# Attention sums and values as 64x32 products, eight side by side, with x in even and odd features

## The chip, the cores and the metric

The kernel runs on one core of one Trainium2 chip. The time is the device time of one execution in microseconds (us). Engines are TensorE (PE; PEld is its weight load), VectorE (DVE), ScalarE (ACT), GpSimd (POOL) and SyncE (SP), which only issues transfers.

## The reference

Windowed attention over 8 batches of 8 heads (576 positions, 64 features), and then a GEGLU feed-forward block over the 8 x 576 = 4608 tokens.

```python
scores = scale * q @ k.transpose(0, 1, 3, 2)            # [8, 8, 576, 576]
mask_plain = (rel >= 0) & (rel < 32)                     # heads 0 to 3
mask_dil = (rel >= 0) & (rel < 128) & (rel % 4 == 0)     # heads 4 to 7
attn = exp(scores - max) / sum                           # under the mask
x = (attn @ v).transpose(0, 2, 1, 3).reshape(4608, 512)
out = (gelu(x @ w_gate) * (x @ w_val)) @ w_out           # d_ff 1536
```

## The kernel before

*Attention.* Two heads form a pair, which fills the 128 partitions; pair n belongs to batch n // 4, and n % 4 is 0 or 1 for plain heads, 2 or 3 for dilated ones. The dilated heads' positions are sorted by their remainder modulo 4, so each head is a narrow band of blocks, 64 keys by up to 96 queries. For a pair these are the steps, each a letter in the kernel's programs:

- **S**: scores, keys on partitions, products of 64x64 tiles (K = 64 features, 64 keys) into PSUM. **P**: exp on ScalarE, of 832 columns for a plain pair and 768 for a dilated one. **M**: times a mask of zeros and ones on VectorE.
- **D**: sums of P over the keys, as products with ones in 64x64 tiles, so that each sum stands in 64 partitions. **N**: values, products with v. Row halves and column halves of the array give four tiles; a word such as `N20@10+N21@40` sends the products of two pairs in turn, so that four tiles can work side by side.
- **l** and **r**: the reciprocal of the sums on ScalarE, as Ln and then Exp of the negative. **X**: values times the reciprocal, on VectorE, into `xT`, the transposed x (features on partitions, four tiles of 128 features, `kc`).

Batch 0 is computed at the start; its first two pairs use 128x128 products with a block-diagonal v (`vdiag`) and block-diagonal ones (`two_ones`), and VectorE turns and inverts their sums (**T**, **B**).

*Feed-forward.* Tokens go in nine chunks of 512. A chunk has a gate phase (`gate_words`) of 96 products of 128x512: 12 blocks of 128 hidden features, each with four gate and four val products over the four `kc`. Gelu (**g**) runs on ScalarE, its product with val (**u**) on VectorE, which in chunks 1 to 8 also forms sums of u blocks (**k**) for a seven-product scheme. The out phase (`out_words`) has 48 products of 128x512 in chunk 0 and 84 of 128x256 in the others, and then **q**, **e** and **w**, which combine and store results through two buffers, `snap`, that lie in `vdiag`. The out phase of chunk c also holds the attention of batch c + 1 for c up to 6; chunks 7 and 8 have none.

*Order.* A program is a string of words; a bare number sends that many feed-forward products to TensorE, any other word sends a step to its engine. Each engine runs its instructions in the order written, and semaphores make it wait. `orders` says in which order the first 16 gate products of a chunk go (three digits: which of the first two blocks, gate or val, kc), so that those which need late parts of x come last. The out phases of chunks 2 to 5 end with the scores of two pairs of the next chunk's batch, so that chunks 3 to 6 find these done; in the out phases of chunks 1 and 2 all scores of their batch are computed.

*Weights.* GpSimd issues the loads of w_gate and w_val (`load_w`, with conversion to 16 bit) in four parts of hidden features, 256, 256, 512 and 512 wide (`WC`). The second pair of heads of batch 0 and the weights come while the start computes.

Of the kernel before, what the change touches and what calls it, by code (L numbers as in the profile page):

```python
# [9 lines left out]
F16 = mybir.dt.float16  # L10
# [11 lines left out]
def kernel(  # L22
# [50 lines left out]
    two_ones = const.tile([P, P], F16, tag="two_ones")  # L73
# [3 lines left out]
    WC = [(0, 256), (256, 512), (512, 1024), (1024, 1536)]  # L77
# [6 lines left out]
    vdiag = const.tile([P, 2 * NB2 * P], F16, tag="vdiag")  # L84
# [9 lines left out]
    snap = [vdiag.bitcast(F32)[:, DM * i : DM * i + DM] for i in range(2)] + [turned[:, 0:DM]]  # L94
# [58 lines left out]
    def load_w(*parts):  # L153

        for i in parts:
            for t, w in ((wg_t, moe_w_gate), (wv_t, moe_w_val)):
                src = w[:, WC[i][0] : WC[i][1]].rearrange("(kc p) n -> p kc n", p=P)
                nc.gpsimd.dma_start(out=t[i], in_=src)
# [35 lines left out]

    diag = vdiag.rearrange("p (e c) -> p e c", c=P)

    def zero():

        for x in range(2):
            nc.vector.memset(at2(vdiag[64 * x : 64 * x + 64].bitcast(F32), 32 - 32 * x, [[64, 2 * NB2], [1, 32]]), 0.0)  # L200
# [32 lines left out]
    def load_v(b, i, plain):  # L233

        st = st_of(i)
        for g in range(2 * plain):
            for x in range(2):
                rows_ = v[b, 2 * g + x].rearrange("(j p) d -> p j d", p=64)
                dst = st[half_of(x, b and g), 576 * g : 576 * g + 576].rearrange("p (j d) -> p j d", j=NB2)
                gated(nc.sync.dma_start(out=dst, in_=rows_))  # L240
        for g in range(2 - 2 * plain):
            for x in range(2):
                half = st[half_of(x, g), 576 * g : 576 * g + 512]
                rows_ = v[b, HK + 2 * g + x, 0 : 4 * P].rearrange("(i p r) d -> p i (r d)", i=2, r=4)
                nc.sync.dma_start(out=half.rearrange("p (i c) -> p i c", i=2), in_=rows_)
        for x in range(2 - 2 * plain):
            dst = st[half_of(x), 512:1152].rearrange("p (g c) -> p g c", c=64)[:, 0:10:9]
            heads = slice(HK + 1, HK + 3) if x else slice(HK, HK + 4, 3)
# [6 lines left out]
    def cast_diag(g):  # L255

        st = st_of(0)[:, 0:1152].rearrange("p (e d) -> p e d", d=D)
        at = slice(NB2 * g, NB2 * g + NB2)
        for x in range(2):
            nc.gpsimd.tensor_copy(diag[half_of(x), at, half_of(x)], st[half_of(x), at])  # L260
# [4 lines left out]

    def odd(n):

        return n % 2 if n >= NHP else 0
# [32 lines left out]
    def cast_part(b, plain, behind=None):  # L301

        ins = cast_v(views(b)[5 - plain], 2 - plain)
        if behind is not None:
            tc.add_manual_dep(ins.ins, behind.ins.name, SYNC, reason="masks first")

    def v_cast(b, g, rest=False):

        dst = views(b)[5][:, NB2 * g : NB2 * g + NB2]
        for x in range(2):  # L310
            half = half_of(x, b and g)
            nc.gpsimd.dma_start(
                out=dst[half, 0:8].rearrange("p (i r) d -> p i (r d)", r=4),
                in_=v[b, HK + 2 * g + x, 0 : 4 * P].rearrange("(i p r) d -> p i (r d)", i=2, r=4),
            )
            if rest:
                heads = slice(HK + x, H, 2)
                if b:
                    heads = slice(HK + 1, HK + 3) if x else slice(HK, HK + 4, 3)
# [5 lines left out]
    def v_cast_plain(b):  # L325

        for g in range(2):
            dst = views(b)[4][:, NB2 * g : NB2 * g + NB2]
            for x in range(2):
                rows_ = v[b, 2 * g + x].rearrange("(j p) d -> p j d", p=64)  # L330
                nc.gpsimd.dma_start(out=dst[half_of(x, g)], in_=rows_)
# [15 lines left out]
    def pair(n):  # L347
        return (n + 2 * (n // NHP in (2, 3))) % NHP

    def is_plain(n):  # L350
        return pair(n) < NHP // 2
# [54 lines left out]
    def win(n, at):  # L406

        bank, kind = at // 10, at % 10
        return 512 * bank + ((0, 832, 960, 0) if is_plain(n) else (80, 880, 880, 64))[kind]

# [33 lines left out]
    def emit(mms):  # L444
        for o, lhs, rhs, st, end in mms:
            nc.tensor.matmul(o, lhs, rhs, start=st, stop=end, skip_group_check=True)  # L446

    def emit_tiles(*lists):

        queues, at = [list(mms) for mms, _ in lists], [0.0] * len(lists)  # L450
        while any(queues):
            i = min((i for i in range(len(lists)) if queues[i]), key=lambda i: at[i])
            o, lhs, rhs, st, end = queues[i].pop(0)
# [23 lines left out]
    def two_s(n, bank):  # L477
# [4 lines left out]
        emit_tiles((two_s_mms(n, bank, not biased), odd(n)))  # L482
# [110 lines left out]
    def two_a(n):  # L593
        two_l(n)
        two_r(n)
# [446 lines left out]
```

## Time and profile before

| | |
|---|---|
| median of 3 runs | 319.06 us (318.95 to 319.46) |
| the profiled execution, its own time | 318.66 us |
| its span, first to last instruction | 317.0 us |
| granted TensorE clock | 1.0 |
| TensorE products | 3489, busy 310.8 us |

The profile comes from one execution; its span leaves out 1.7 us of that execution's own time. "PE" rows count a product from its start to its modelled end, so neighbours overlap; distances are read from start to start. A row such as `PE L457 MATMUL ps<-q 64*64 64x96 f16 x36` is 36 products at line 457, tile shape 64x64, the first of 96 columns. A few per cent of matmul records can be missing or counted with a neighbour.

### The profile page before, as it was taken

The numbers are of one execution on the slowest core, as the hardware profiler recorded it, in microseconds if no ns is written. First come the engines' busy times: TensorE is split into PE (matmuls) and PEld (weight loads), VectorE is DVE, ScalarE is ACT, GpSimd is POOL, SyncE is SP. The second block draws the span as 40 slices with busy tenths as digits, with TensorE's granted clock in tenths as the row PEclk, the third lists the DMA queues.
The fourth block names the chain that finished last, engine by engine and source line by source line (L and its number), as shares of the span: only waits on it lengthen the run. The fifth ranks groups of instructions, "written<-read, shape, count | busy, mean of one in ns | idle before, by whom it ended". The sixth has DMA issues, their size and how long they took to land.

```text
span 317.0 us, 8449 instructions
## 1 busy us (share of the span) xinstructions
PE 310.8 (98%) x3489; PEld 184.0 (58%) x3489; DVE 211.4 (67%) x368; ACT 164.2 (52%) x248; POOL 85.2 (27%) x134
## 2 busy tenths in 40 slices
PE   7999999999999999999999999999999999999995
PEld 4854545446854586448644774478446844674474
DVE  6863656799865786788667676768566756626542
ACT  2673476535763476338733774367536753334330
POOL 8884703412466150333135021511000000000000
PEclk9999999999999999999999999999999999999999
DMA  8999997897799998989789667974100210030003
GB/s 189 184 198 206 206 198 145 259 191 194 159 286 181 203 201 145 251 207 198 188 228 245 150 173 178 246 171 125 35 0 2 77 60 1 0 106 28 0 2 132
DMA packets 110790, 47.15 MB, mean 149 GB/s; under 512 B 83616, under 2 KB 110240, under 8 KB 110752
## 3 DMA queue, kind: packets, MB, share of 16 engines
q1 hardware_dynamic: 97248, 38.29, 53.4%
q0 software_dynamic: 12944, 7.67, 17.2%
q10 hardware_dynamic: 560, 0.66, 0.8%
q8 instruction: 27, 0.44, 0.6%
q14 instruction: 11, 0.09, 0.1%
HBM read 37.75 MB, written 9.44 MB: 149 GB/s over the span
## 4 chain that ended last, share of the span: by engine, by line
PE 94%; DMA 2%; DVE 2%; ACT 1%; POOL 0%; issue 0%
PE ps L622 59%; PE ps L704 23%; PE ps L457 6%; PE ps L629 3%; DMA xT<-in_q_dram 2%; PE ps L377 1%; DVE P L492 1%; ACT P L487 1%; DVE xT L613 0%; PE ps L796 0%; PE ps L446 0%; PE ps L397 0%; DVE vdiag L742 0%; ACT rb L590 0%; POOL band L122 0%
## 5 line engine op out<-in xcount | busy, mean ns | idle before, releaser
L905 ACT ACTIVATE g<-ps 128x512 f16<-128x512 f32 x108 | 64.3, 597 | 100.9 <-PE ps L622 100.8
L910 DVE SCALAR_TENSOR_TENSOR u_all<-g,ps 128x512 f16<-128x512 f16 x108 | 73.9, 686 | 63.9 <-PE ps L622 46.4
L622 PE MATMUL ps<-xT,wv 128*128 128x512 f16 x432 | 112.5, 379 | 0.0
L622 PE MATMUL ps<-xT,wg 128*128 128x512 f16 x432 | 111.5, 379 | 0.3 <-DMA wg<-in_moe_w_gate_dram 0.2
L622 PEld LDWEIGHTS <-wg 128*128 128x128 f16 x432 | 42.2, 98 | 50.6 <-DMA wg<-in_moe_w_gate_dram 0.3
L622 PEld LDWEIGHTS <-wv 128*128 128x128 f16 x432 | 42.3, 98 | 49.8 <-issue 0.4
L704 PEld LDWEIGHTS <-u_all 128*128 128x128 f16 x390 | 36.6, 98 | 6.5 <-issue 0.3
L704 PE MATMUL ps<-wo,u_all 128*128 128x256 f16 (+1 forms) x294 | 35.5, 271 | 0.0
L704 PE MATMUL ps<-wx,ux 128*128 128x256 f16 x288 | 35.1, 273 | 0.0
L613 DVE TENSOR_TENSOR xT<-ps,rb 128x576 f16<-128x576 f32 x32 | 29.1, 938 | 4.8 <-PE ps L457 3.3
L487 ACT ACTIVATE P<-ps 128x832 f16<-128x832 f32 (+1 forms) x32 | 25.3, 835 | 11.5 <-PE ps L457 11.4
L704 PEld LDWEIGHTS <-ux 128*128 128x128 f16 x288 | 27.7, 98 | 3.8
L253 POOL CAST v<-stage 128x1152 f16<-128x1152 f32 x11 | 12.9, 1176 | 62.6 <-DMA stage<-in_v_dram 43.9
L216 POOL CAST s<-stage 128x640 f16<-128x640 f32 x24 | 17.9, 774 | 43.4 <-DMA stage<-in_q_dram 31.0
L665 DVE TENSOR_TENSOR ux<-u_all 128x512 f16<-128x512 f16 x48 | 22.0, 457 | 1.6
L584 ACT ACTIVATE lg<-ps 128x576 f32<-128x576 f32 x30 | 18.8, 655 | 7.5 <-PE ps L457 4.2
L590 ACT ACTIVATE rb<-lg 128x576 f32<-128x576 f32 x30 | 19.0, 688 | 0.1
L228 POOL CAST s<-stage 128x512 f16<-128x512 f32 x24 | 15.9, 693 | 10.6 <-DMA stage<-in_q_dram 8.7
L670 DVE TENSOR_TENSOR ux<-u_all,ux 128x512 f16<-128x512 f16 (+1 forms) x32 | 14.6, 456 | 1.1
L672 DVE TENSOR_TENSOR u_all<-ux,u_all 128x512 f16<-128x512 f16 (+1 forms) x32 | 12.4, 386 | 0.9
L729 DVE SCALAR_TENSOR_TENSOR part<-ps,vdiag 128x512 f32<-128x512 f32 x15 | 10.3, 687 | 3.3 <-PE ps L704 3.3
L704 PE MATMUL ps<-wx,u_all 128*128 128x256 f16 x96 | 11.8, 273 | 0.0
(84 smaller groups left out, 228.2 us busy)
## 6 DMA issues: line engine op xcount, KB each, us to landing
out_dram<-part SPq DMA_DIRECT2D x30, 256.0 KB, 3.1
stage<-in_v_dram SPq DMA_DIRECT2D x28, 144.0 KB, 3.7
stage<-in_q_dram SPq DMA_DIRECT2D x24, 128.0 KB, 3.6
stage<-in_k_dram SPq DMA_DIRECT2D x24, 128.0 KB, 2.9
stage<-in_q_dram SPq DMA_DIRECT2D x6, 512.0 KB, 4.7
stage<-in_k_dram SPq DMA_DIRECT2D x6, 512.0 KB, 5.5
stage<-in_v_dram SPq DMA_DIRECT2D x20, 128.0 KB, 2.9
wo<-in_moe_w_out_dram POOLq DMA_DIRECT2D x3, 512.0 KB, 16.5
```

Of the source, the lines that this page charges most:

```text
L216: nc.gpsimd.tensor_copy(s16[:, 1280 * t + 640 * g : 1280 * t + 640 * g + 640].rearrange("p (k c) -> p k c", k=5), st_of(i).rearrange("p (k ...
L228: nc.gpsimd.tensor_copy(s16[:, at : at + 512].rearrange("p (r h d) -> p h r d", r=4, h=2), st_of(i)[:, 512 * g : 512 * g + 512].rearrange( ...
L457: nc.tensor.matmul(o[cols], lhs[rows], rhs[rows], start=st, stop=end, skip_group_check=True)
L487: nc.scalar.activation(pt[:, 0 : src.shape[1]], src, AF.Exp, bias=0.0, scale=scale)
L584: nc.scalar.activation(lg, psf[:, c0 : c0 + S], AF.Ln)
L590: nc.scalar.activation(rb, tiles.pop(("lg", n)), AF.Exp, scale=-1.0)
L613: nc.vector.tensor_tensor(dst, num, rb, ALU.mult)
L622: nc.tensor.matmul(ps[:, bank, :], w[:, kc, ns], xT[kc][:, tok], start=first, stop=end)
L665: nc.vector.tensor_tensor(ux[:, j, 0:2], k0, u_all[:, 2 * j : 2 * j + 2, hi], ALU.subtract)
L704: lambda o=o, s=s[:, P * p : P * p + P], t=t[:, c0:c1], st=st, end=end: nc.tensor.matmul(o, s, t, start=st, stop=end, skip_group_check=True)
L905: nc.scalar.activation(g, ps[:, gate_banks(c, args[0])[0], :], AF.Gelu)
L910: nc.vector.scalar_tensor_tensor(u_all[:, nb, :], tiles.pop(("g", nb)), -USCALE if c in SEVEN and nb % 2 else USCALE, val, ALU.mult, ALU.mult)
```

## The change

Sums and values are now products of 64x32 tiles: a tile takes one head's half of the partitions and writes 32 partitions, and four heads (two pairs) fill the 128 output partitions. `emit_tiles` places pair n's head x in the 32 columns g = 2 (n % 2) + x; the dilated heads use the other row half, so plain and dilated tiles never share one, and a word with four pairs has eight tiles in turn. Sums of a four take 20 (plain) or 24 (dilated) products. Values run twice, with the even features of v (`e:D:2`, e = 0) and the odd ones: 160 to 164 products per batch for 80 to 84. `xT[kc]` then holds the even (kc 0, 2) or odd (kc 1, 3) features of four heads, plain (0, 1) or dilated (2, 3), and `load_w` loads rows of the weights to match: `load_w(i, q)` loads half of the features, 256 rows, of part i, and `WC` has three parts of 512.

One Ln and one Exp serve four heads, so two of each per batch instead of four. `vdiag`, `two_ones` and their set-up are gone; batch 0's v is cast whole (`cast_first_v`), only the first four heads' sums are inverted on VectorE, and `snap` has its own memory.

```diff
-                rows, cols = half_of(x), half_of(x, lists[i][1])
+                rows, cols, st = half_of(x), half_of(x, swap), first
+                if kind != "S":
+                    g = 2 * (n % 2) + x
+                    rows, cols, st = cols, slice(32 * g, 32 * g + 32), (first, g) not in opened
+                    opened.add((first, g))
                 nc.tensor.matmul(o[cols], lhs[rows], rhs[rows], start=st, stop=end, skip_group_check=True)
...
-        ones_of = two_ones if n < NHP else ones[:, 0:BK]
+        ones_of = ones[:, 0:32]
...
+            return two_mms(n, w0, lambda j: vp[:, NB2 * hp + j, e:D:2])
+        return two_mms(n, w0, lambda j: vd[:, NB2 * hp + (8 if j is None else j % 2 * 4 + j // 2), e:D:2])
...
-    def two_x(n):
-        rb, c0 = tiles["rb", n], tiles["num", n]
-        dst, num = xT[pair(n)][:, rows_of(n)], psf[:, c0 : c0 + S]
+    def two_x(four, e):
+        rb, c0 = tiles["rb", four], tiles["num", four, e]
+        dst, num = xT[four % 2 * 2 + e][:, rows_of(2 * four)], psf[:, c0 : c0 + S]
...
-    WC = [(0, 256), (256, 512), (512, 1024), (1024, 1536)]
+    WC = [(0, 512), (512, 1024), (1024, 1536)]
...
-    def load_w(*parts):
-        for i in parts:
-            for t, w in ((wg_t, moe_w_gate), (wv_t, moe_w_val)):
-                src = w[:, WC[i][0] : WC[i][1]].rearrange("(kc p) n -> p kc n", p=P)
-                nc.gpsimd.dma_start(out=t[i], in_=src)
+    def load_w(i, q):
+        for t, w in ((wg_t, moe_w_gate), (wv_t, moe_w_val)):
+            src = w[2 * P * q : 2 * P * q + 2 * P, WC[i][0] : WC[i][1]].rearrange("(p e) n -> p e n", e=2)
+            nc.gpsimd.dma_start(out=t[i][:, 2 * q : 2 * q + 2], in_=src)
```

The stages are written anew. Each of the chunks 1 to 6 now has one form: the scores of pairs i and k (the first plain and the first dilated one) in the gate phase, late, between feed-forward products; the other two pairs' scores in the out phase; then all four sums in one block, and all values in another:

```diff
-            return (
-                f"{open_} S{k}@1+S{l}@4 D{i}@11+D{j}@41 P{k} P{l} {6 if c < 3 else 4} q2@0 M{k} M{l}{v1} 12 l{i} l{j} r{i} r{j} q3@0 "
-                f"12 N{i}@10+N{j}@40 D{k}@12+D{l}@42 q4@0 X{i} l{l} X{j} l{k} r{l} r{k} 12 q5@0 {8 if c < 3 else 4} "
-                f"N{k}@13+N{l}@43 {after} X{l} X{k} {4 if c < 3 else 8}"
-            )
+        sums_ = f"D{i}@1472+D{j}@1472+D{k}@2928+D{l}@2928"
+        values = [f"N{i}@{a}@{e}+N{j}@{a}@{e}+N{k}@{b}@{e}+N{l}@{b}@{e}" for e, a, b in ((0, 512, 2112), (1, 1472, 2928))]
         return (
+            f"E P{i} P{k} 1 u11 k5@0 k5@1 11 q0@0 M{i} k5@2 M{k} 12 q1@1 2 S{j}@1+S{l}@4 P{j} P{l} M{j} 10 q2@1 M{l} "
+            f"12 {sums_} q3@0 l{p} l{d} r{p} r{d} 12 q4@0 1 {values[0]}+{values[1]} X{p}@0 X{d}@0 G 11 q5@0 X{p}@1 X{d}@1 12"
```

Chunk 0's out phase has four blocks: two of scores, one of all four sums, then the values of e = 0 and, 8 products later, those of e = 1.

TensorE, the first rows of a value block in chunk 3's out phase (`v` is one buffer of values, `P_` one pair's exponentials). Before:

```order
L457 MATMUL ps<-P_2449,v_104 64x96
L457 LDWEIGHTS v_104
L457 MATMUL ps<-P_2449,v_104 64x96
L457 LDWEIGHTS v_104
L457 MATMUL ps<-P_2451,v_104 64x96
L457 LDWEIGHTS v_104
L457 MATMUL ps<-P_2451,v_104 64x96
```

After:

```order
L430 LDWEIGHTS v_101
L430 MATMUL ps<-P_2781,v_101 32x96
L430 LDWEIGHTS v_101
L430 MATMUL ps<-P_2781,v_101 32x96
L430 LDWEIGHTS v_101
L430 MATMUL ps<-P_2855,v_101 32x96
L430 LDWEIGHTS v_101
L430 MATMUL ps<-P_2855,v_101 32x96
L430 LDWEIGHTS v_101
L430 MATMUL ps<-P_2783,v_101 32x96
L430 LDWEIGHTS v_101
L430 MATMUL ps<-P_2783,v_101 32x96
```

Four tiles of 64 columns, from two pairs, came before the next block of keys; now eight of 32 columns from four pairs do.

VectorE in chunk 5's out phase (L742 copies a partial result, L492 and L465 are M, L628 is a sum of u blocks, L729 and L685 combine and store, L613 and L569 are X). Before:

```order
L492 TENSOR_TENSOR P_3501<-P_3501,two_p 128x832
L492 TENSOR_TENSOR P_3503<-P_3503,two_p 128x832
L742 TENSOR_SCALAR turned<-ps 128x512
L492 TENSOR_TENSOR P_3610<-P_3610,two_d 128x768
L492 TENSOR_TENSOR P_3612<-P_3612,two_d 128x768
L729 SCALAR_TENSOR_TENSOR part<-ps,turned 128x512
L729 SCALAR_TENSOR_TENSOR part<-ps,vdiag 128x512
L613 TENSOR_TENSOR xT_99<-ps,rb 128x576
L613 TENSOR_TENSOR xT_100<-ps,rb 128x576
L729 SCALAR_TENSOR_TENSOR part<-ps,vdiag 128x512
L613 TENSOR_TENSOR xT_102<-ps,rb 128x576
L613 TENSOR_TENSOR xT_101<-ps,rb 128x576
```

After:

```order
L465 TENSOR_TENSOR P_3961<-P_3961,two_p 128x832
L628 TENSOR_TENSOR u_all<-ux,u_all 128x256
L465 TENSOR_TENSOR P_3963<-P_3963,two_d 128x768
L465 TENSOR_TENSOR P_4035<-P_4035,two_p 128x832
L465 TENSOR_TENSOR P_4037<-P_4037,two_d 128x768
L685 SCALAR_TENSOR_TENSOR part<-ps,turned 128x512
L685 SCALAR_TENSOR_TENSOR part<-ps,snap_114 128x512
L569 TENSOR_TENSOR xT_96<-ps,rb 128x576
L569 TENSOR_TENSOR xT_98<-ps,rb 128x576
L685 SCALAR_TENSOR_TENSOR part<-ps,snap_113 128x512
L569 TENSOR_TENSOR xT_97<-ps,rb 128x576
L569 TENSOR_TENSOR xT_99<-ps,rb 128x576
```

All four masks now stand close together ahead of the stores, and a copy (into `turned`) has left the stretch. ScalarE at the same place (P, Ln and Exp are L487, L584 and L590 before, L460, L544 and L550 after), before:

```order
L937 ACT_TABLE_LOAD
L487 ACTIVATE P_3501<-ps 128x832
L487 ACTIVATE P_3503<-ps 128x832
L738 ACTIVATE vdiag<-ps 128x512
L487 ACTIVATE P_3610<-ps 128x768
L487 ACTIVATE P_3612<-ps 128x768
L584 ACTIVATE lg<-ps 128x576 x2
L590 ACTIVATE rb<-lg 128x576 x2
L584 ACTIVATE lg<-ps 128x576 x2
L590 ACTIVATE rb<-lg 128x576 x2
L738 ACTIVATE part<-ps 128x512
L939 ACT_TABLE_LOAD
```

After:

```order
L893 ACT_TABLE_LOAD
L460 ACTIVATE P_3961<-ps 128x832
L460 ACTIVATE P_3963<-ps 128x768
L694 ACTIVATE snap_114<-ps 128x512
L460 ACTIVATE P_4035<-ps 128x832
L460 ACTIVATE P_4037<-ps 128x768
L694 ACTIVATE turned<-ps 128x512
L544 ACTIVATE lg<-ps 128x576 x2
L550 ACTIVATE rb<-lg 128x576 x2
L895 ACT_TABLE_LOAD
L694 ACTIVATE part<-ps 128x512
```

Four Ln and four Exp became two and two, and the copy into `turned` came to ScalarE between the last P and the first Ln.

GpSimd at the start, the loads of the first weights and the casts of batch 0's v. Before:

```order
L158 DMA wg_88<-in_moe_w_gate_dram 128x4x256
L158 DMA wv_92<-in_moe_w_val_dram 128x4x256
L158 DMA wg_89<-in_moe_w_gate_dram 128x4x256
L158 DMA wv_93<-in_moe_w_val_dram 128x4x256
L260 CAST vdiag<-stage 64x9x64 x4
L158 DMA wg_90<-in_moe_w_gate_dram 128x4x512
```

After:

```order
L155 DMA wg_87<-in_moe_w_gate_dram 128x2x512
L155 DMA wv_90<-in_moe_w_val_dram 128x2x512
L155 DMA wg_87<-in_moe_w_gate_dram 128x2x512
L155 DMA wv_90<-in_moe_w_val_dram 128x2x512
L248 CAST v_100<-stage 128x576 x2
L155 DMA wg_88<-in_moe_w_gate_dram 128x2x512
```

A pair of loads carried all features of 256 columns; now it carries half the features (the kc 0 and 1, then 2 and 3) of 512 columns.

The first 16 gate products of chunk 0 go `000 010 001 011 100 110 101 111 003 013 103 113 002 012 102 112` by the table, which was `000 100 002 102 010 110 012 112 001 101 011 111 003 103 013 113`.

More of the change, by code (lines that the diff above doesn't have):

```diff
@@ L299, in load_rest, with cast_part @@
                 cast_part(b, part)
[L301 to L305, printed above, removed]
+    def cast_part(b, plain):
+        cast_v(views(b)[5 - plain], 2 - plain)
     def v_cast(b, g, rest=False):
@@ L481, in two_s @@
             bias_first(n, bank)
-        emit_tiles((two_s_mms(n, bank, not biased), odd(n)))
+        emit_tiles((two_s_mms(n, bank, not biased), n, "S"))
     def two_p_of(n):
@@ L823 @@
     biases()
-    zero()
     bias_first(0, 4)
+    load_w(0, 0)
     load_w(0, 1)
     for g in range(2):
-        cast_diag(g)
-    load_w(2)
+        cast_first_v(g)
+    for part in range(2):
+        load_w(1, part)
     def second():
-        load_w(3)
+        for part in range(2):
+            load_w(2, part)
         for src, t in zip((q, k), nine):
```

169 lines of the change are left out of this document (61 added, 108 removed), and 14 rows, old and new, of tables (at, orders).

## The prediction

> **What bounds the kernel now.** I read the page's busy line and chain first, then the span by stages, then TensorE's order inside a stage.
>
> ```profile
> PE 310.8 (98%) x3489; PEld 184.0 (58%) x3489; DVE 211.4 (67%) x368; ACT 164.2 (52%) x248; POOL 85.2 (27%) x134
> ...
> PE 94%; DMA 2%; DVE 2%; ACT 1%; POOL 0%; issue 0%
> ```
>
> TensorE is busy 98% of the span and is 94% of the chain that ended last. Time is won only by giving TensorE less to do or less to wait for; the halved Ln and Exp on ScalarE are worth nothing unless somebody waits for them. The stages are chunk 0's gate phase, its out phase, then chunks 1 to 7 (columns: stretch, length, then busy time of PE, PEld, DVE, ACT, POOL; the clock is the 1.00).
>
> ```profile
> 18.50:41.29 22.79, 22.75 (x231) 10.86 (x230) 12.15 (x18) 10.98 (x20) 14.14 (x30) 1.00 1.25 204
> 41.29:55.28 13.99, 13.98 (x246) 7.07 (x246) 7.57 (x11) 9.23 (x13) 2.96 (x4) 1.00 1.02 169
> 55.28:88.90 33.62, 33.38 (x377) 19.92 (x376) 29.20 (x52) 18.73 (x28) 10.33 (x13) 1.00 0.88 205
> 88.90:122.51 33.61, 33.61 (x413) 20.14 (x412) 23.37 (x40) 18.73 (x28) 15.37 (x24) 1.00 1.31 206
> 122.51:155.48 32.97, 32.97 (x389) 19.87 (x388) 24.50 (x41) 18.68 (x28) 8.71 (x12) 1.00 0.87 198
> 155.48:188.31 32.83, 32.83 (x389) 19.76 (x388) 22.42 (x41) 18.69 (x28) 9.96 (x13) 1.00 0.83 211
> 188.31:221.14 32.83, 32.83 (x389) 19.76 (x388) 23.76 (x41) 18.68 (x28) 8.42 (x11) 1.00 0.72 177
> 221.14:253.58 32.44, 32.44 (x353) 19.38 (x352) 21.88 (x40) 18.68 (x28) 0.00 (x0) 1.00 0.09 30
> 253.58:283.55 29.97, 29.97 (x181) 17.63 (x180) 16.83 (x31) 10.84 (x17) 0.00 (x0) 1.00 0.10 33
> ```
>
> Chunk 7 carries no attention: 29.97 is the price of one chunk's feed-forward part. What a chunk has above it is what this change edits: 3.65 in chunk 1, 2.86 in chunks 4 and 5, 2.47 in chunk 6.
>
> **What one attention block costs.** TensorE in chunk 5's out phase, and two pieces of the chain (start, us, matmuls):
>
> ```profile
> 212.45 0.54 PE L457 MATMUL ps<-q 64*64 64x96 f16 x36
> 212.82 0.56 PE L457 MATMUL ps<-P,ones 64*64 64x96 f16 x28
> 213.31 0.61 PE L704 MATMUL ps<-wx,ux 128*128 128x256 f16 x4
> ...
> 219.19 0.57 PE L457 MATMUL ps<-P,v 64*64 64x96 f16 x44
> 219.62 0.54 PE L457 MATMUL ps<-q 64*64 64x96 f16 x36
> ...
> 219.27 0.89 PE ps L457 x79
> ...
> 274.38 9.17 PE ps L704 x84
> ```
>
> Start to start, the scores of two head pairs take 0.37 (212.45 to 212.82), values 0.43 (219.19 to 219.62); a feed-forward product of 256 columns takes 9.17/84 = 0.109. Chunk 0's out phase shows what entering and leaving tiles costs:
>
> ```profile
> 41.96 2.98 PE L629 MATMUL ps<-wo,u_all 128*128 128x512 f16 x13
> 44.87 0.56 PE L457 MATMUL ps<-q 64*64 64x96 f16 x36
> 45.37 2.12 PE L629 MATMUL ps<-wo,u_all 128*128 128x512 f16 x9
> 47.41 0.54 PE L457 MATMUL ps<-P,ones 64*64 64x288 f16 x24
> 47.88 3.19 PE L629 MATMUL ps<-wo,u_all 128*128 128x512 f16 x14
> 51.01 0.55 PE L457 MATMUL ps<-P,v 64*64 64x96 f16 x40
> ...
> 51.89 2.33 PE L629 MATMUL ps<-wo,u_all 128*128 128x512 f16 x10
> 54.16 0.58 PE L457 MATMUL ps<-P,v 64*64 64x96 f16 x40
> 54.67 0.60 PE L629 MATMUL ps<-wo,u_all 128*128 128x512 f16 x2
> ```
>
> A 512-column product takes 0.216 (two of 0.109 bound it at 0.218; eight that stand with the start take 1.72). Thirteen from 41.96 end at 44.77; the scores start at 44.87 and the next product at 45.37: a block of scores alone costs 0.60, some 0.19 of it the two changes of tile shape. The same sum gives sums alone 0.57, values and sums together 0.99, values alone 0.62.
>
> **The change, part by part.**
>
> *Sums and values in 64x32 tiles.* Four heads' sums now stand eight tiles side by side, where two head pairs stood four abreast. If eight run at once, the sums of a batch take 0.40 instead of 0.38 twice, one block of 0.59 with the switches. Values stream every column twice (even features, then odd), each pass with all four head pairs abreast: 2 x 0.43 = 0.86, no more than before, 1.06 with the switches. The program has 658 matmuls more. No row of before has eight tiles abreast, so the bounds: nothing gained beyond some 5% of a block, since the same columns stream; at worst the tiles run four at a time, and then the sums stay at 0.76 and the values double to 1.72. I take the low end. In the last fence, 36 scores over 832 columns (S4 and S5) take 0.50 (44.87 to 45.37) and 24 sums over 768 columns (D6 and D7) 0.47 (47.41 to 47.88); the 64 columns between them are 64/512 x 0.216 = 0.03, so twelve matmuls more cost next to nothing, and columns set the time. Against it: the closest that matmuls start in a tiled block is 0.89/79 = 11 ns, and eight abreast over 96 columns (40 ns) would need 5.
>
> The Trainium skill, "TensorEngine Tiling (Array Packing)", section "Instruction Overhead", speaks against this edit: it gives each matmul about 60 cycles whatever its free dimension and advises against tiling a dimension that is already small, as the 64 features here. At one column a cycle, 512 in 0.216 us are 2.4 cycles per ns, and 60 of them are an estimate of 25 ns each, against the trace's 11; by the rule 658 more would come to 16 us. The trace disagrees so far.
>
> *Chunks 1 to 6.* All get the same stages: scores of two pairs early in the gate phase 0.60, the others alone in the out phase 0.60, sums 0.59, values 1.06: 29.97 + 2.85 = 32.82, now in four blocks. Against the rows: chunk 1 -0.80, chunk 2 -0.79, chunk 3 -0.15, chunks 4 and 5 0, chunk 6 +0.38. Together -1.4. Chunk 1 also loses this stall:
>
> ```profile
> 80.28 0.23 PE L457 MATMUL ps<-P,ones 64*64 64x96 f16 x2
> 80.75 0.55 PE L457 MATMUL ps<-P,ones 64*64 64x96 f16 x22 [0.24 <-DVE P L492]
> ```
>
> It is in chunk 1's 0.80: two sums took 0.47 until the masked P came.
>
> *Chunk 0's out phase.* 48 products at 0.216 are 10.36; scores 2 x 0.60, sums 0.58, values 2 x 0.62 make 13.38; I add 0.1 for the last masks. 13.99 becomes 13.5: -0.5 (-0.3 to -0.6).
>
> *The start.* Before, TensorE enters the gate phase like this (TensorE, then VectorE, then the last of the first four weight transfers):
>
> ```profile
> 17.68 0.39 PE L622 MATMUL ps<-xT,wg 128*128 128x512 f16 x1 [0.18 <-DMA wg<-in_moe_w_gate_dram]
> ...
> 21.78 1.89 PE L622 MATMUL ps<-xT,wg 128*128 128x512 f16 x8
> 23.50 0.81 PE L622 MATMUL ps<-xT,wv 128*128 128x512 f16 x3
> ...
> 16.35 0.72 DVE L613 TENSOR_TENSOR xT<-ps,rb 128x576 f16<-128x576 f32 x1
> 17.36 2.98 DVE L613 TENSOR_TENSOR xT<-ps,rb 128x576 f16<-128x576 f32 x3 [0.29 <-ACT rb L590]
> ...
> L158 POOL DMA_DIRECT2D wv<-in_moe_w_val_dram x1: 750/750/750, 13.3 to 13.3; - x1
> ...
> DMA to landing us min/median/max: 7.7/8.0/8.3
> ```
>
> Sixteen gate products end at 21.78 and need only the first two weight transfers, all features of 256 columns. After, a transfer holds half the features of 512 columns; products 10 to 16 need the fourth, which before was issued at 13.28 and landed 8.3 later, at 21.58. If it keeps its place, the sixteenth ends at 21.5 + 7 x 0.216 = 23.0. The four normalisations agree: the first now needs values of both plain pairs, which I put at 18.0; two of 0.72 and two of some 1.1 (2.98 less 0.72, halved) end at 21.7, and four products behind it at 22.6. I take +1.2, bounds +0.3 (the halves read 2 KB pieces instead of 1 KB, so may land earlier) and +1.6.
>
> *New waits in the stages.* One block of sums now needs all four masks; before, two. Chunk 5's other engines, ScalarE's first two exponentials, its last Ln and Exp, and VectorE's last two masks:
>
> ```profile
> 210.11 1.62 ACT L487 ACTIVATE P<-ps 128x832 f16<-128x832 f32 x2
> ...
> 217.56 1.44 ACT L584 ACTIVATE lg<-ps 128x576 f32<-128x576 f32 x2 [0.54 <-PE ps L457]
> 218.90 1.25 ACT L590 ACTIVATE rb<-lg 128x576 f32<-128x576 f32 x2
> ...
> 214.56 1.02 DVE L492 TENSOR_TENSOR P<-P,two_d 128x768 f16<-128x768 f16 x2
> ```
>
> The second scores now stand after 26 products of 0.109 (2.83 into the out phase), these are done at 3.4, their two exponentials 1.6 later, about 5.1, and the last mask half a us behind that, at 5.7. TensorE reaches the sums after 48 products and the scores: 48 x 0.109 + 0.60 = 5.83. Cover 0.1: a mask that is slowed, as chunk 1's was, shows fully. Behind the sums (done at 6.4) stand two Ln and two Exp, 2.6 from 217.56 to 220.15: 9.0; the values are done by then (13 products after the sums, then 1.06). Four normalisations (3.6 by the start's rows above) and a store's sum between them, for which I take 0.7, end at 13.3. TensorE leaves the out phase at 84 x 0.109 + 0.60 + 0.59 + 1.06 = 11.4 and has nine gate products of the first three features (1.9) before it needs the last: 13.3. Cover zero. For both I put +0.3 in six chunks, bounds 0 and +2.8 (0.47 each, the stall above).
>
> *At nothing.* The moved copy (q2 to ScalarE) and halved Ln and Exp: ScalarE is 52% busy and does the copy while the sums are still to come. If the cover goes, the copy's 0.6 delays an Ln by as much, and through the normalisations the gates. The identity work for the diagonal of v and its zeroing leave VectorE and GpSimd before the start's first casts; what waits there is x's transfers. GpSimd's queue now issues the first four transfers in the same place with the same bytes, then eight halves.
>
> **The sum.** +1.2 - 0.5 - 1.4 + 0.3 = -0.4, on the profiled execution of 318.66: 318.3. The median of the runs, 319.06, lies 0.4 above it: **318.7**. About 0.2% (0.64) is what a measurement of this kernel can tell from no change: 318.4 to 319.7 is "same".
>
> **Rivals.**
>
> 1. *Faster, 317.4.* The halves land early and normalisation is the start's only limit (+0.6), no new wait in the stages (0), tiles a little better than four abreast (-0.05 in each of seven batches): 0.6 - 0.5 - 1.4 - 0.35 = -1.65. For it: 94% of the chain is TensorE, so waits were mostly planned out. Against: the fourth transfer's 21.58.
> 2. *Slower, 320.8: the sums wait for the last mask.* In each of chunks 1 to 6 VectorE ends the fourth mask 0.4 after TensorE arrives: 2.4 instead of 0.3. It decides from the point where masks end later than 5.83 + 0.2 into the out phase. For it: chunk 1's stall of this kind. Against: GpSimd's casts of v move away from the masks in chunks 4 to 6.
> 3. *Slower: eight tiles don't run abreast.* If 11 ns from start to start is a limit, a batch's values (82 matmuls more, so some 164) take 1.80 instead of 0.86 and its 44 sums 0.48 instead of 0.40: 1.02 x 7 = 7.1 more, 325.8. If only four tiles run together, it is (0.86 + 0.36) x 7 = 8.5: 327.2. For it: no row with eight. Against: columns, not matmuls, set the time above.
> 4. *Slower: a fixed fee on each of the 658 matmuls.* At the 25 ns of a serial issue it is 16.5: 335. The 11 ns starts speak against it. (The rule of the page named above is of this kind.)
>
> **Chances.** Forecast (318.4 to 319.7) 0.37; first rival 0.35; second 0.18; third 0.08; fourth 0.02. Faster 0.35, same 0.37, slower 0.28. The range 316.8 to 321.8 leaves out the third and fourth and a few hundredths at the ends of the first two.
>
> **What would show it.** In the profile after: tiles of the sums and values in 64*32 form; the values' block from its first start to the next product 1.0 to 1.1 (1.9 or 2.0 is rival 3); chunks 1 to 6 each at 32.8, chunk 6 longer than before; chunk 0's out phase near 13.5; the sixteenth gate product of chunk 0 ending near 23.0, with a wait on the val weights; sums without an idle time behind a mask. It is wrong if tiles of 32 columns load their weights more slowly than those of 64, or if the start's weights or a normalisation in every chunk come later than worked out.

## The result, and the profile after

The changed kernel took 332.9 us (332.7 to 335.9, four runs) where the kernel before took 319.2 beside it: a ratio of 1.045 (95% interval 1.039 to 1.051). The profiled execution took 333.06, its span is 331.4 against 317.0. The forecast was 318.7, within 0.2% of no change; the measured time is 11 us above its range. Here and below, an execution that took over 1.5% longer than the fastest of its kernel, at a lower granted clock, is left out.

The page's parts that answer to those of before: the busy line, the instruction queue and the chain. The second fence is the instruction queue's row of before.

```profile
PE 314.0 (95%) x4147; PEld 185.8 (56%) x4147; DVE 206.3 (62%) x352; ACT 149.6 (45%) x225; POOL 86.1 (26%) x136
...
q8 instruction: 32, 0.52, 0.7%
...
PE 88%; DMA 4%; issue 3%; DVE 3%; SPq 1%; ACT 0%; POOL 0%; POOLq 0%
```

```profile
q8 instruction: 27, 0.44, 0.6%
```

TensorE has 658 products more but is busy only 3 us longer (314.0 for 310.8). The other 11 us are idle time, and the chain has a new entry, 3% "issue": time in which an engine waited for nothing that the profile shows. Who waited for whom, TensorE's lines (us in all, times, longest):

```profile
PE ps L430 <- issue: 7.4, 7, 2.3
...
PE ps L660 <- issue: 1.1, 1, 1.1
PE ps L660 <- DVE snap L698: 0.9, 1, 0.9
PE ps L578 <- issue: 0.7, 1, 0.7
...
PE ps L430 <- DVE P L465: 0.4, 1, 0.4
```

Nine waits of the "issue" kind, 9.2 us in all; before there was none in this list. The list counts from the modelled end of the product before; from start to start the nine pauses cost 11.0. The stages, in the columns used before:

```profile
20.33:44.43 24.10, 23.29 (x233) 10.98 (x232) 13.12 (x19) 9.73 (x18) 15.03 (x31) 1.00 1.23 200
44.43:58.75 14.32, 14.14 (x325) 7.25 (x325) 6.54 (x9) 9.63 (x13) 3.82 (x5) 1.00 0.86 165
58.75:94.17 35.42, 33.69 (x461) 20.08 (x460) 27.86 (x51) 16.28 (x24) 14.32 (x22) 1.00 0.85 206
94.17:129.15 34.98, 33.71 (x463) 20.10 (x461) 23.29 (x39) 16.88 (x25) 9.89 (x15) 1.00 1.25 185
129.15:163.63 34.48, 33.40 (x462) 19.97 (x460) 24.49 (x41) 16.88 (x25) 10.00 (x13) 1.00 0.84 200
163.63:198.26 34.63, 33.59 (x462) 20.09 (x460) 22.48 (x38) 16.88 (x25) 8.64 (x11) 1.00 0.74 167
198.26:234.01 35.75, 33.41 (x462) 20.05 (x460) 24.21 (x40) 16.88 (x25) 8.46 (x11) 1.00 0.68 163
234.01:267.94 33.93, 33.41 (x463) 20.01 (x461) 21.13 (x39) 16.88 (x25) 0.00 (x0) 1.00 0.10 32
267.94:297.83 29.89, 29.89 (x183) 17.62 (x181) 17.28 (x32) 9.55 (x16) 0.00 (x0) 1.00 0.11 36
```

Chunk 7, without attention, is unchanged (29.89). Each of the chunks 1 to 6 is 1.1 to 2.9 longer than the 32.8 forecast, and chunks 2 to 6 differ by up to 1.8 although TensorE's words in them are the same. Two out phases show why: chunk 5's, with a pause (TensorE's order, and then the value block's stretch with line 430 alone), and chunk 3's, whose value block has none:

```profile
225.50 0.58 PE L430 MATMUL ps<-P,ones 64*32 64x64 f16 x44
226.01 1.49 PE L660 MATMUL ps<-wx,ux 128*128 128x256 f16 x12
227.34 0.27 PE L660 MATMUL ps<-wo,u_all 128*128 128x256 f16 x1
227.54 1.50 PE L430 MATMUL ps<-P,v 64*32 64x96 f16 x161
231.37 0.19 PE L430 MATMUL ps<-P,v 64*32 64x16 f16 x3 [2.33 <-issue]
231.49 2.69 PE L660 MATMUL ps<-wo,u_all 128*128 128x256 f16 x23
```

```profile
227.50:228.86 1.36, 1.32 (x161) 1.29 (x162) 1.00 0.49 159
```

```profile
158.22 0.27 PE L660 MATMUL ps<-wo,u_all 128*128 128x256 f16 x1
158.43 1.51 PE L430 MATMUL ps<-P,v 64*32 64x96 f16 x164
159.87 2.47 PE L660 MATMUL ps<-wo,u_all 128*128 128x256 f16 x21
```

The sums are as forecast: 0.51 start to start and 0.1 to enter, 0.6 in all. The values are not. In chunk 5, 161 products start within 1.31, from the 33rd on one every 8.4 ns; eight side by side over 96 columns would be 40 ns, and they take 67. Then TensorE stands still for 2.33 (2.52 from start to start) with three products of the block left. The block without a pause, in chunk 3, its two changes of shape with it, costs 159.87 - 158.22 - 0.11 = 1.54, where 1.06 was forecast.

### The profile page after: what moved, and what is told of

Read it like the earlier page. It is cut to its first block, busy times and chain, and to the rows that moved or that the text cites. A ratio compares the mean times of both kernels' runs of the same rounds, so it can differ in the third digit from the quotient of the medians.

```text
span 331.4 us, 9705 instructions
## 1 busy us (share of the span) xinstructions
PE 314.0 (95%) x4147; PEld 185.8 (56%) x4147; DVE 206.3 (62%) x352; ACT 149.6 (45%) x225; POOL 86.1 (26%) x136
## 4 chain that ended last, share of the span: by engine, by line
PE 88%; DMA 4%; issue 3%; DVE 3%; SPq 1%; ACT 0%; POOL 0%; POOLq 0%
PE ps L578 56%; PE ps L660 21%; PE ps L430 7%; PE ps L585 3%; DMA stage<-in_v_dram 2%; DMA u_all<-in_q_dram 2%; SPq L230 1%; DVE u_all L866 1%; DVE ux L621 1%; DVE P L465 0%; DVE xT L569 0%; PE ps L353 0%; DVE ux L626 0%; ACT P L460 0%; PE ps L373 0%
## 5 line engine op out<-in xcount | busy, mean ns | idle before, releaser
L569 DVE TENSOR_TENSOR xT<-ps,rb 128x576 f16<-128x576 f32 x32 | 28.6, 934 | 19.5 <-PE ps L430 19.5
L460 ACT ACTIVATE P<-ps 128x832 f16<-128x832 f32 (+1 forms) x32 | 25.3, 834 | 6.2 <-PE ps L430 5.4
L621 DVE TENSOR_TENSOR ux<-u_all 128x512 f16<-128x512 f16 x48 | 23.6, 492 | 1.7
L430 PE MATMUL ps<-P,v 64*32 64x96 f16 (+5 forms) x1304 | 14.3, 201 | 7.8 <-issue 7.4
L430 PEld LDWEIGHTS <-v 64*32 64x32 f16 x1304 | 12.0, 90 | 11.3 <-issue 10.4
L685 DVE SCALAR_TENSOR_TENSOR part<-ps,snap 128x512 f32<-128x512 f32 x15 | 10.3, 688 | 9.5 <-PE ps L660 9.4
L694 ACT ACTIVATE part<-ps 128x512 f32<-128x512 f32 x7 | 4.2, 597 | 24.1 <-PE ps L660 24.1
L628 DVE TENSOR_TENSOR u_all<-ux,u_all 128x512 f16<-128x512 f16 (+1 forms) x32 | 13.6, 426 | 0.9
```

Source lines behind the costliest of these rows:

```text
L430: nc.tensor.matmul(o[cols], lhs[rows], rhs[rows], start=st, stop=end, skip_group_check=True)
L460: nc.scalar.activation(pt[:, 0 : src.shape[1]], src, AF.Exp, bias=0.0, scale=scale)
L569: nc.vector.tensor_tensor(dst, num, rb, ALU.mult)
L621: nc.vector.tensor_tensor(ux[:, j, 0:2], k0, u_all[:, 2 * j : 2 * j + 2, hi], ALU.subtract)
L628: nc.vector.tensor_tensor(k0[:, :, hi], ux[:, at, 2], k1[:, :, lo], ALU.subtract)
```

## The experiments

Counting TensorE's weight loads and products from the start of the trace, all nine pauses of the changed kernel end at a place that leaves 193 when divided by 256. Two theories of mine rest on that. **F**: TensorE's program reaches it in blocks of 256 instructions (the instruction queue's row: 32 packets, 0.52 MB, so 16 KB each; 32 x 256 = 8192 for its 8294 loads and products, and 27 packets for the 6978 of before), and a block used up quickly leaves the next one late. **I**: a weight load or product is issued only every 4.2 ns, once a stock of some 32 products in TensorE's queue is used up. The rival, **P**: the pauses and the slow values belong to 64x32 tiles or to places in the program.

**Shifting the program.** Two kernels move every TensorE instruction by 120 places, one forward, one back, through the warm-up ahead of the first data:

```diff
-    warm(69, 7, 32, 32)
-    warm(4, 7)
+    warm(133, 7, 32, 32)
```

> The changed kernel, with 60 small products more in TensorE's warm-up at the very start (64 of 32 columns in place of four of 512, about as long), so that every later TensorE instruction stands 120 places further on in the program; nothing else changes. Theory F (instruction fetch: TensorE's program arrives in blocks of 256 instructions, and where two blocks are used up faster than about 9 to 13 us the next is late): the idle times put down to 'issue' stay at places 193 modulo 256 of the instruction count and so move 60 products earlier in the code: in chunk 5 from behind value product 161 of 164 to about 101, in chunk 2 from 133 to 73, in chunk 4 from 109 to 49. Time 330 to 335. Theory P (they belong to the place: a PSUM bank, a semaphore, the reads of the exponentials): they stay behind the same products, and the time stays within 0.5 of 332.9.

```diff
-    warm(69, 7, 32, 32)
+    warm(9, 7, 32, CH // 2)
     warm(4, 7)
```

> The changed kernel with 60 products fewer in TensorE's warm-up (9 of 256 columns in place of 69 of 32, about as long), so that every later instruction stands 120 places further ahead in the program. Theory F: the idle times stay at 193 modulo 256 and move 60 products later in the code; the start's second one (behind the 14th gate product) moves into the long gate products, where it is hidden, and the first into the value block; the sixteenth gate product ends at 22 to 24 instead of 24.9; in chunks 1 to 6 the closest pairs of blocks are 6.9, 7.3, 8.3 and 8.5 us, so these still lose 1.5 to 2.5 each: 329 to 333. If the start is held by its transfers or normalisations, the sixteenth ends at 24.9 as before this edit.

Measured: 339.5 forward (ratio 1.062, 1.059 to 1.065) and 333.3 back (1.044, 1.041 to 1.047). The places of the pauses of over 0.25 us from start to start (plain changes of tile shape and waits for another engine left out), counted in each trace:

```
changed kernel   705  961 1985 2753 3777 4801 5569 6593 7361   all 193 modulo 256
shift forward    705  961 3009 4801 5825 6593 7617             all 193 modulo 256
shift back       449  705 2753 4545 5569 6337 7361             all 193 modulo 256
```

The pauses keep to the count and leave the code: shifted forward, chunk 5's moved from behind value product 161 to 101, as expected. Those of chunks 2 and 4 did not come at 73 and 49 (0.1 us at the one, nothing at the other); the two blocks that end there took 12.6 and 15.6 us, and 8.9 and 11.6 in the changed kernel. Theory P falls. What I missed: the total forward (330 to 335 expected; the time back lies just above its range), and the start in both. Shift forward, TensorE and then a stretch with its clock; behind them TensorE with the shift back:

```profile
18.53 0.27 PE L430 MATMUL ps<-P,v 64*32 64x96 f16 x12 [0.21 <-ACT lg L544]
21.71 0.67 PE L430 MATMUL ps<-P,v 64*32 64x96 f16 x46 [2.90 <-issue]
```

```profile
21.70:28.00 6.30, 6.27 (x60) 2.55 (x60) 2.82 (x3) 0.00 (x0) 3.76 (x7) 0.52 1.23 202
```

```profile
21.36 0.64 PE L430 MATMUL ps<-P,v 64*32 64x96 f16 x54 [2.90 <-issue]
```

In both, nearly all of the start's pauses came as one of 2.9, and TensorE's granted clock was low behind it: 0.52 over the 6.3 us that follow in the first. So the sixteenth gate product started later (28.3 and 26.8) than the changed kernel's 24.7. With the shift forward the clock was also 0.5 for 3.4 us each from 96.06 and from 270.14, at the ends of pauses of 2.7 and 2.5; chunks 1 and 6, where they lie, took 38.1 and 37.4 for 35.4 and 33.9. These two chunks and the start are where the kernel shifted forward lost more than the changed kernel. The Trainium skill, "TensorE: Matmul & The Clock Gate", section "What's actually happening", puts the idle window after which the clock halves at about 3.4 us. Here pauses of 2.5 to 2.9 were enough (1.9 in the run with one value pass, below), while the changed kernel's of 2.3 was not followed by it.

**The packets behind the pauses.** The trace holds every packet of the instruction queue, 16384 bytes each. For the nine pauses of the changed kernel, in us:

```
last block began    12.64  18.84  53.07  87.21  123.66  158.88  191.75  227.79  261.31
packet, start       16.47  22.19  53.79  88.65  123.88  160.78  192.49  228.75  262.08
packet, end         17.44  23.17  55.32  89.68  124.83  162.14  193.73  229.92  263.21
pause ends          18.84  24.48  56.59  90.89  126.38  163.41  195.21  231.37  264.69
```

Between the place where the last block began (193 modulo 256 as well) and the pause's end there is one packet, and TensorE goes on 1.2 to 1.6 us after it has ended. In the traces of the other versions the pauses end 1.2 to 1.8 us behind a packet too. Together with the places this makes them waits for blocks of instructions.

**As many instructions in chunks 1 to 6, without the new tiles.** The kernel before, each value block of these chunks issued twice:

```diff
-                f"12 N{i}@10+N{j}@40 D{k}@12+D{l}@42 q4@0 ...
+                f"12 N{i}@10+N{j}@40 N{i}@10+N{j}@40 D{k}@12+D{l}@42 q4@0 ...
```

(and `N{k}@13+N{l}@43` likewise).

> The kernel before, with every value block of chunks 1 to 6 issued twice (64x64 tiles as they were, the second pass overwrites the first): as many instructions per batch as the changed kernel, none of its tiles. Theory F: idle times put down to 'issue' appear at every 256th instruction where blocks follow fast, 2 to 6 us in all, beside 6 x 2 x 0.43 = 5.2 for the doubled values: 326 to 330. If 64x32 tiles are what is slow: 5.2 alone, 324.3, without such idle times.

Measured: 329.6 (1.032, 1.027 to 1.036), inside the first range. TensorE in its chunk 4, and its waits:

```profile
189.63 0.98 PE L457 MATMUL ps<-P,v 64*64 64x96 f16 x80
190.43 0.53 PE L457 MATMUL ps<-P,ones 64*64 64x96 f16 x24
...
192.75 0.89 PE L457 MATMUL ps<-P,v 64*64 64x96 f16 x74
194.54 0.28 PE L457 MATMUL ps<-P,v 64*64 64x80 f16 x13 [0.90 <-issue]
```

```profile
PE ps L457 <- issue: 3.4, 4, 1.1
...
PE ps L457 <- DVE P L492: 1.4, 2, 0.7
```

The pauses come with 64x64 tiles too, at places 2497, 3521, 4289, 5313 and 6337: 193 modulo 256 again, when the few semaphore instructions that this program has among TensorE's are counted with them. Late masks (the second line) add to the time, so the total alone would not decide. And 80 products of 64 columns start within 0.78, 80 of 32 columns in the changed kernel's chunk 0 (below) within 0.63: 9.9 and 8.0 ns a product, so halving a tile's width bought a fifth and not half.

**One value pass less.** The changed kernel without the odd features' values in chunks 1 to 6:

```diff
-  ... 12 q4@0 1 {values[0]}+{values[1]} X{p}@0 X{d}@0 G 11 q5@0 X{p}@1 X{d}@1 12"
+  ... 12 q4@0 1 {values[0]} X{p}@0 X{d}@0 G 11 q5@0 X{p}@1 X{d}@1 12"
```

> The changed kernel without the odd features' values in chunks 1 to 6 (the odd features get the even ones' values; batches 2 to 7 are computed so): 80 to 82 products fewer per batch, all else as it was. Theory F plus I: a value block of 0.76 instead of 1.5 (-4.4 in six chunks) and nearly no late instruction block in these chunks (-6 to -7.8): 321 to 323. If the idle times have another cause than the number of instructions: 328.

Measured: 330.6 (1.034, 1.031 to 1.037), only 2.4 below the changed kernel's profiled 333.1, far above the range and above the other theory's 328 too. The pauses did go, from nine to five and from 9.2 to 5.4, none later than 161 us. A wait took their place:

```profile
PE ps L578 <- DVE xT L569: 4.4, 9, 0.6
PE ps L430 <- issue: 3.2, 2, 1.9
...
PE ps L660 <- issue: 1.2, 2, 0.9
PE ps L578 <- issue: 1.0, 1, 1.0
```

The next chunk's gate products now wait for the normalisations. In its chunks 2 to 6 the stages take 33.9 to 34.0 although TensorE's work, without these waits, is near 32.6. Chunks 5 and 6 have no pause at all and still take 34.0. So the cover that I had put at zero for this chain is about 1.1 short: even without late blocks these stages would not come down to 32.8. Chunk 1 took 36.8, with a pause of 1.9 and the clock at 0.5 for 3.4 us behind it.

**Two blocks of values, or five.** First, 8 feed-forward products between the even and the odd features' values; then 2 after every 32 value products:

```diff
-  1 {values[0]}+{values[1]} X{p}@0 X{d}@0 G 11 q5@0
+  1 {values[0]} X{p}@0 X{d}@0 8 {values[1]} G 3 q5@0
```

> The changed kernel, with the values of the even and of the odd features of chunks 1 to 6 in two blocks, 8 feed-forward products (0.87 us) between them, as chunk 0 has it already. Theory F plus I (I: past the first 32 products, TensorE starts a weight load or product only every 4.2 ns): a block of 80 takes 0.76 as in chunk 0, two of them as much as the one of 1.5, the two more changes of tile shape cost 0.19, which the refilled queue gives back; the late instruction blocks shrink by up to 0.87 in most chunks, 3 to 5 in all: 328 to 330. If the lost time were in the 64x32 tiles themselves: 333 to 334.

```diff
             at[i] += max(int(np.prod(rhs.shape[1:])), 72)
+            if between is not None and sent % 32 == 0 and 0 < sent < 160:
+                between()      # two feed-forward products
+            sent += 2
```

> The changed kernel with two feed-forward products after every 32 value products of chunks 1 to 6 (five pieces with four gaps in place of one block; the same products in all). Theory I (32 products are queued up and run at the pace of the columns, what follows at 4.2 ns per instruction): a piece of 32 takes 0.17 to 0.2, so that the block's own time falls from 1.5 to 0.9, and eight more changes of tile shape (0.8) eat it up; theory F: the late blocks shrink by up to 0.9 each. Together 327 to 330. If 64x32 tiles were slow by themselves, a piece takes 0.3 and the time is 332 to 334.

Measured: 333.3 (1.043, 1.040 to 1.046) and 336.5 (1.054, 1.049 to 1.059): both ranges missed on the slow side, the first at the rival's figure. In the first the pauses did shrink, to 2.3 us in three, but the second block now waits until X has read the first one's values:

```profile
PE ps L430 <- DVE xT L569: 4.5, 6, 0.8
PE ps L430 <- issue: 2.1, 2, 1.7
...
PE ps L578 <- issue: 0.2, 1, 0.2
```

That wait is the edit's own, and the run can't tell the theories apart. In the second, chunk 5's pieces show the pace:

```profile
231.70 0.36 PE L434 MATMUL ps<-P,v 64*32 64x96 f16 x32
231.99 0.39 PE L664 MATMUL ps<-wo,u_all 128*128 128x256 f16 x2
```

A piece of 32 goes from 231.70 to the next product at 231.99: 0.29, of which some 0.1 is the change of shape, so 6 ns a product where the long block needs 8.4. This fits theory I (a stock of some 32 products runs at the columns' pace; the rest come at the pace of issue). What sets that pace, the issuing or the loads of weights themselves, no run tells. Eight more changes of shape cost more than that brought, and in its list of waits the late blocks kept 7.4 us and gate products waited for X; the clock is also at 0.5 for 3.4 us behind chunk 1's pause of 2.0:

```profile
PE ps L434 <- issue: 5.9, 5, 2.0
PE ps L582 <- DVE xT L573: 2.0, 5, 0.4
...
PE ps L664 <- issue: 0.8, 1, 0.8
PE ps L582 <- issue: 0.7, 1, 0.7
```

**The kernel before, shifted.** By 60 places, and then by 30:

```diff
-    warm(69, 7, 32, 32)
-    warm(4, 7)
+    warm(101, 7, 32, 32)      # the other run: warm(85, 7, 32, 32); warm(3, 7)
+    warm(2, 7)
```

> The kernel before with 30 small products more in the warm-up (32 of 32 columns in place of two of 512, about as long): every later TensorE instruction stands 60 places further on, no other edit. Theory F: the closest two blocks of 256 instructions, 10.3 to 13.6 us in chunks 2 to 5 before, become 8.8 to 9.9 us, close to those that were late elsewhere: three or four idle times of 0.3 to 1 appear at places 193 modulo 256, 320 to 322 in all. If the count of instructions is no cause: 318.8 to 319.4, no such idle times.

> The kernel before with 15 small products more in the warm-up: every later TensorE instruction stands 30 places further on (the earlier shift was 60). By the trace of before the closest two blocks then take 8.2, 8.3 and 9.0 us, in chunks 5, 4 and 3. Theory F with the earlier runs (two blocks were late when used within 7.7 to 9.0 us outside the start): idle times at 193 modulo 256 of 0.3 to 0.9 in each of these chunks, 320 to 321.5. If alignment is no cause: 319.1 to 319.5 without them.

Measured: 320.0 to 322.0 in four executions (ratio 1.006, 1.004 to 1.008), and 320.0 to 322.8 in three, 318.8 being the kernel before beside them. The totals lie near what was expected, but for another reason. The first trace has one pause at 193 modulo 256, of 0.29; the second has none. Both begin with a delay: the longer warm-up puts off the first gate product by 0.6, and a copy in chunk 1 makes TensorE wait for 0.5. Two blocks used within 8.2 us did not pause there, so my bound on two blocks was wrong. Both profiled executions took 320.0, the low end of their runs, and what the longer ones lost is open. I don't count these two as evidence for F.

**The early scores alone.** The kernel before, with chunk 1's and 2's first scores in the gate phase and the words of chunks 3 to 5:

```diff
+        if c < 3:
+            early[8 if c == 1 else 7] += f" S{NHP * (c + 1)}@12+S{NHP * (c + 1) + 1}@15"
...
-            if c < 3:
-                open_ = f"1 u11 k5@0 7 S{i}@1+S{j}@4 E P{i} P{j} k5@1 4 q0@0 k5@2 M{i} M{j} 12 q1@1 6"
```

> The kernel before with one part of the change alone, the early scores: in chunks 1 and 2 too the scores of the first two pairs stand in the gate phase (before, inside the out phase), and these chunks get the words that chunks 3 to 5 have; tiles, values, reciprocals and weights as before. Theory: chunks 1 and 2 then cost what chunks 4 and 5 do, 32.8 in place of 33.6, and the masked exponentials are no longer late in chunk 1: -1.4 to -1.6, 317.6 to 318.2 (ratio 0.995). Rival: other waits (the casts of v beside the masks of chunk 1) keep half of it: 318.5 to 319.

Measured: 320.4 (1.0045, 1.0026 to 1.0063): 0.45% slower, a miss.

```profile
79.74 1.03 PE L704 MATMUL ps<-wx,ux 128*128 128x256 f16 x8 [0.59 <-DVE vdiag L742]
...
89.81 1.02 PE L622 MATMUL ps<-xT,wv 128*128 128x512 f16 x4 [0.60 <-DVE xT L613]
```

I had reasoned badly: a block of scores costs its 0.6 wherever it stands, and in chunks 1 and 2 a copy on VectorE and the normalisations (this batch has its dilated pairs first, which the order of gate products that I gave these chunks didn't follow) then made TensorE wait.

**The start alone.** The changed kernel without the odd values of batch 0:

```diff
-  X0@0 N1@3072@1+N2@1104@0+N3@1104@0 X0@1 X1@1 X1@0
+  X0@0 N2@1104@0+N3@1104@0 X0@1 X1@1 X1@0
```

(its two other odd words left out likewise).

> The changed kernel without the odd features' values of batch 0 (its odd features get the even ones' values): 80 products fewer at the start, nothing else. Theory F: the block at place 705 still comes at about 18.3 to 18.8 and stops the values; the next boundary, 961, falls behind some 90 gate products and is hidden; the sixteenth gate product ends at about 23.3, 1.4 before the changed kernel's 24.7. If the transfers of the weights or the normalisations hold the start, it ends at 23.9 or later with a wait put down to them. In chunks 1 to 6 the idle times move by 160 places and sum to 5 to 9: 329 to 333.

It took 333.8, above the range; its profile is of a longer execution, of 339.0, so I take no time from it. What doesn't hang on the time: the pause at place 705 stayed and none stood at 961, as expected, and no gate product waited for a weight transfer. No experiment measures the transfers' share of the start apart from the blocks'.

## Why the prediction was wrong

The step that failed is "Sums and values in 64x32 tiles", at "twelve matmuls more cost next to nothing, and columns set the time". What the runs showed in its place: TensorE pays for the number of instructions, in two ways.

*The pace of values* (forecast 0.86 for two passes, 1.06 with the switches; measured 1.54 where no pause falls in the block). In the two rows that I compared, 36 scores and 24 sums, products start 11 and 16 ns apart. That is slower than the 8.4 ns above, so there the columns do set the time, and the rows could not show the limit. Chunk 0's out phase shows both sides of it:

```profile
52.98 0.83 PE L430 MATMUL ps<-P,v 64*32 64x96 f16 x80
53.74 1.90 PE L585 MATMUL ps<-wo,u_all 128*128 128x512 f16 x8
55.57 0.85 PE L430 MATMUL ps<-P,v 64*32 64x96 f16 x59
56.59 0.28 PE L430 MATMUL ps<-P,v 64*32 64x80 f16 x21 [0.17 <-issue]
```

One pass of 80 takes 0.76, or 0.66 without the change of shape behind it, not 0.43. Within it the first 32 products start between 52.98 and 53.14, 42 ns for eight; the last 48 between 53.22 and 53.61, 67 ns for eight. Over chunks 1 to 6 this is 6 x 0.48 = 2.9. The rival of the 11 ns spacing had the right kind of mechanism (a pace per product) with too high a price, 1.80 for 1.33; I had given it 0.08. Its 11 ns was not the closest spacing on record either: the row of 44 values that I read beside it, 0.43 long, gives 9.8.

*The late blocks* (forecast nothing; measured 11.0 from start to start, 7.9 of it in chunks 1 to 6). No step of the prediction asked how instructions reach TensorE. The row of the instruction queue stood on the page of before (27 packets) and was not read: 658 products more are 1316 instructions, five blocks more, and nearly all in bursts. That the blocks are the cause is shown by the shifts, by the doubled values and by the packets: pauses follow the count, with tiles of both shapes, and end 1.2 to 1.8 us behind a packet. Where they came, a block followed the one before by 2.7 to 5.5 us in the chunks and by 5.1 to 6.5 at the start, while the value block uses one up in 256 x 4.2 ns = 1.1 us. By the table above, the changed kernel's chunks spend this time so: 0.2 to 1.9 until the packet starts, 0.9 to 1.5 for the packet, 1.2 to 1.6 until TensorE goes on. At the start the packets begin only 3.4 to 3.8 after the boundary. Whether other transfers hold them back there was not tested. They aren't needed for a pause: in chunk 6 with the shift forward the packet took 0.9, as short as any, and the pause was 2.5. Why a packet starts when it does stays open, and so does why some blocks that were used just as fast (2.8 us in chunk 2 with the shift forward) came in time.

The other steps, by the profiles:

- *Chunks 1 to 6.* Forecast -1.4 and +0.3 for new waits; measured +10.9 (209.2 for 198.3). From start to start the parts are the forecast -1.4, values 2.9, pauses 7.9 and waits for VectorE 1.6 (1.0 for a copy in chunk 1, 0.6 for a mask in chunk 4), 11.0 in all. The second rival, late masks, was a small part of the truth. In chunk 5 a mask's neighbour on VectorE did slow down (1.23 us for a sum of 0.29) while GpSimd cast v beside it, and the mask stayed in time by 0.2.
- *Sums eight abreast:* right. 44 products, 0.6 with the switches in chunk 5; their columns are many and their instructions few.
- *Chunk 0's out phase.* Forecast 13.5, measured 14.32. The two value passes cost 0.85 (52.98 to 53.74, and 0.1 to enter) and, with a pause in it, 1.32, where 0.62 each was forecast. No wait for a mask came.
- *The start.* Forecast +1.2, the sixteenth gate product ending at 23.0; it started at 24.70 for 21.56 before, +3.1, and ended at 24.91. The reason named did not occur: no gate product waited for a weight transfer. Two pauses did, among the values (below) and behind the fourteenth gate product (0.73), 2.7 together from start to start:

```profile
16.97 0.23 PE L430 MATMUL ps<-P,v 64*32 64x96 f16 x6 [0.32 <-POOL v L248]
18.84 1.13 PE L430 MATMUL ps<-P,v 64*32 64x96 f16 x114 [1.64 <-issue]
20.33 0.38 PE L578 MATMUL ps<-xT,wg 128*128 128x512 f16 x1 [0.36 <-DVE xT L569]
```

- *At nothing:* ScalarE's halved Ln and Exp and the moved copy. ScalarE's busy time fell by 15 us, and TensorE never waited for it. This was not tried by itself.
- *The normalisations' cover of zero:* about 1.1 us too much in each chunk, by the run with one value pass. In the changed kernel the slower values and the pauses hide it; as soon as they shrink (one pass, five pieces) the gate products wait, 4.4 and 2.0.

The fourth rival's figure, 335, is close to the measured time by chance: its fee of 25 ns per product is three times the 8.4 that the trace shows, and most of the loss is pauses. The fee was an estimate after the Trainium skill, "TensorEngine Tiling (Array Packing)", section "Instruction Overhead". The advice of that section, not to tile a dimension that is already small, agrees with the result. Another page bears on this case, and the prediction did not use it: the Trainium skill, "Runtime: NRT & Kernel Launch", section "Instruction fetch mechanics", says that instructions are refilled in blocks of 16 KiB, 256 instructions, fetched while the block before is executed. The trace agrees on the size of the block; that the cost is mostly hidden, as the section adds, holds for the kernel before and not for the changed one.

None of the versions tried is faster than the kernel before.

## What to carry to other kernels

Count instructions as well as columns: here a burst of 64x32 products ran at the pace of its columns only for the first 32 or so, then at 8.4 ns for each load and product. When a change raises TensorE's count, see how fast the busiest stretches use up 256 instructions. Where a block was used in under some 3 to 5 us the next one was often late, though not always; in the kernel before, where none took less than 4.4, all came in time. The mark is "issue" in the list of waits at a fixed step of the instruction count, with a packet of the instruction queue that ends shortly before. Splitting a tile's columns to lay more tiles side by side pays only where each still streams enough columns to cover that pace; at 96 columns and eight tiles it did not.

## What was not expected of the hardware

Chunks in which TensorE has the same words differed by up to 1.8 us (33.93 to 35.75) because a block boundary fell elsewhere in them, and 60 small products more at the very start, in time that was idle anyway, moved the whole kernel from 333 to 339. A pause in the instruction stream can also cost the clock: behind pauses of 2.9, 2.7 and 2.5 us in that run it was granted at 0.5 for 6.8, 3.4 and 3.4 us.
